# Sparse attention and a SiLU feed-forward layer on one Trainium2 core: batch 3's preparation at the places of batch 2, its four x transposes from ScalarE

## The chip, the cores and the metric

The kernel runs on one core of a Trainium2 chip. Its engines are TensorE (PE, with PEld for the loading of weights), VectorE (DVE), ScalarE (ACT), GpSimd (POOL) and SyncE (SP, which here only issues DMAs). An engine name with a q (ACTq, SPq) is that engine's instruction queue, where the issuing of a DMA shows. The metric is device time in microseconds (us) of one execution. All times "in the trace" are counted from the start of the profiled execution's span.

## The reference, cut to what matters

Four batches, 8 heads, 768 positions, head size 64. Each position attends to the keys less than 16 positions away and to 24 block keys (the maximum over 32 keys), whose values are block means; the output goes through a feed-forward layer with SiLU.

```python
k_sum = k.reshape(B, H, nb, block, D).max(axis=3)      # block 32, nb 24
v_sum = v.reshape(B, H, nb, block, D).mean(axis=3)
scores_l = scale * np.matmul(q, k.transpose(0, 1, 3, 2))
mask_l = np.abs(pos[:, None] - pos[None, :]) < 16
scores_s = scale * einsum(q, k_sum) + np.log(block)
a = softmax(concatenate([where(mask_l, scores_l, -1e9), scores_s]))
x = np.matmul(a, concatenate([v, v_sum]))              # (3072, 512)
h = x @ w_in                                           # 512 -> 2048
out = (h * sigmoid(beta * h)) @ w_out                  # 2048 -> 512
```

## The kernel before, in words

The batches go one after the other, and each has two **stages** on PE. The *h stage* is `x @ w_in` (16 tiles of 128 features, L600), with ACT's Silu behind each tile (L611). The *product stage* is the product with `w_out`, done by a seven-product scheme (L664, products numbered 1 to 7) for three row tiles t = 0, 1, 2: 21 products of 8 matmuls each. VectorE makes sums of h for it (L645).

The attention of batch b is **prepared inside the product stage of batch b-1**, in pieces slipped between the products. Heads are worked in four pairs, g = 0 to 3. The pieces, with their names in the table `AT` that gives their places, are:

- `exp`: a tiny Exp on a dummy tile that brings ACT's exp table in (L743), and `silu`, the same for the Silu table (L740); `ACT_TABLE_LOAD` in the trace.
- `sc`: 24 score matmuls for a pair and a half of the positions (L436), into `big[2]` or `big[1]`, then ACT's exp of them into a tile `e` (L447).
- `mk`: VectorE's multiplication of `e` with the window mask (L451).
- `vm`: 28 matmuls that make the block sums of v (L486) into the bank `scope["c"]` (acc in the trace), with small copies by DVE and ACT to `vm_sb`.
- `sp`: the spread, copies of `vm_sb` into the value tiles `ve` and `vo`; for pairs 0 and 1 by DVE (L371), for 2 and 3 by ACT (L368).
- `av`: 48 matmuls for a pair (L511) into `big[1]` (g even) or `big[2]` (g odd), then DVE's normalization into `xn` (L537, L538).
- `xd`: the transpose of `xn` into `xT`, by a DMA (L553). The table `xq` chooses who issues it: a number above 0 SP, a number from -1 to 0 ACT.

The bank `one[0]` is worth knowing: products 1 and 2 are accumulated in it, ACT copies each result out (L368: `p<-one` for product 1, `o_sb<-one` for product 2), and the h stage puts its tile 3 into `one[0]` and `one[1]` (the first matmuls of line 600 that write `one`).

```python
587     def h_bank(i, kk):
...
589         if i == 3:
590             return one[kk][:, 0, 0:HS]
...
690         elif n == 2:
691             part["lo"] = op.tile([P, d_model], f32, name="o_sb", tag="o_sb")
692             act_cp(part["lo"][:, 0:DH], src)
```

The order is written out by hand. `main` is a list of PE's steps: the h steps of batch 2 are 84 to 99, its products 100 to 120, and batch 3's h steps begin at 121. The products of batch 1 are 63 to 83, so a place of batch 2's preparation plus 37 is the same place for batch 3. `AT` gives each piece a number, and `run` slips it in behind the step of that whole number; between pieces of one step the smaller number goes first.

```python
553         (nc.sync if AT[f"xq{b}"][g] > 0 else nc.scalar).dma_start_transpose(...)
...
747         for i, f in enumerate(main):
748             f()
749             while sides and sides[0][0] < i + 1:
750                 sides.pop(0)[1]()
```

Every engine takes its instructions strictly in this written order. The recording layer adds the semaphore waits. A DMA's completion is a semaphore called DMAHW0 to DMAHW7, taken in turn by the DMAs of SP and ACT.

Of the kernel before, what the change touches and what calls it, by code (L numbers as in the profile page):

```python
# [65 lines left out]
    'qd3': [91.148, 91.216, 90.659, 93.011],  # L66
    'vc3': [95.284, 91.652, 97.814, 103.191],
    'vo3': [97.047, 94.075, 98.896, 104.362],
    'exp3': [100.49],
    'sc3': [101.05, 101.06, 104.012, 104.199, 106.253, 106.263, 107.654, 107.71],  # L70
    'mk3': [102.2, 102.9, 107.921, 107.97, 106.952, 108.221, 108.907, 110.666],
    'silu3': [112.501],
    'vm3': [107.308],
    'sp3': [107.454, 109.9, 110.9],
    'av3': [110.088, 110.664, 114.187, 114.973],
    'xd3': [111.756, 114.644, 117.265, 117.799],
    'hs3': [126.972, 131.206, 132.732, 134.708, 136.323],
    'xq1': [-0.443, -0.159, -0.972, -0.722],
    'xq2': [-0.681, -0.396, -0.684, -0.009],
    'xq3': [-0.996, -0.83, 0.5, -0.341],  # L80
    'mask2': [46.27],
}

# [887 lines left out]
```

## Time and profile before

| | us |
|---|---|
| median of 3 runs | 212.68 (211.92 to 213.24) |
| the profiled execution, its own time | 211.17 |
| its span, first to last instruction | 209.5 |
| PE busy | 201.5 (96%) |
| DVE, ACT, POOL busy | 138.2, 124.8, 64.0 |

The granted TensorE clock was 0.992 on average. The profile's view of the chain of waits follows the work that ended last back from the end of the span, and names at each step what released it. The timeline view gives start and duration of each group of like instructions of an engine; a bracket behind it gives the idle time ahead of it and what ended that.

### The profile page before, as it was taken

The page shows a single profiled execution, that of the slowest core. Times are in us where ns is not written, and L with a number is a line of the kernel's source. Part 1 is how long each engine was busy: PE and PEld are TensorE (multiplying, and loading weights), DVE is VectorE, ACT ScalarE, POOL GpSimd, SP SyncE. Part 2 cuts the span into 40 slices and gives each one's busy share as a digit, 9 for nine tenths or more (in the row PEclk, how much of TensorE's full clock was granted, in tenths as well). Part 3 has the DMA queues.
Part 4 walks back from the last instruction along what each step waited for, and adds up shares of the span by engine and source line. Part 5 has one row for each costly group of instructions (what it writes and reads, how often), then busy time and mean ns, then how long its engine had stood idle before and what let it go on. Part 6 is the DMA issues. An engine that isn't in the chain of part 4 may idle for free.

```text
span 209.5 us, 5777 instructions
## 1 busy us (share of the span) xinstructions
PE 201.5 (96%) x2387; PEld 139.8 (67%) x2387; DVE 138.2 (66%) x314; ACT 124.8 (60%) x189; POOL 64.0 (31%) x95
## 2 busy tenths in 40 slices
PE   7899999999999999999999999999999899999993
PEld 2478656656455775556888865568788656568882
DVE  4568674899889981859999523999699304464132
ACT  2438876689777114867978229669895039662210
POOL 7708990101820036530520072453501100000111
PEclk9969999999999999999999999999999999999999
DMA  6999999999969999999989979999525530000242
GB/s 121 190 223 170 181 187 188 207 207 202 184 160 231 228 227 258 226 175 206 129 217 242 201 211 288 178 200 189 133 96 102 150 103 3 0 0 3 100 100 100
DMA packets 79193, 34.12 MB, mean 163 GB/s; under 512 B 61488, under 2 KB 76224, under 8 KB 79168
## 3 DMA queue, kind: packets, MB, share of 16 engines
q1 hardware_dynamic: 62768, 24.12, 56.4%
q0 software_dynamic: 7424, 7.34, 22.0%
q10 hardware_dynamic: 8976, 2.30, 7.6%
q8 instruction: 18, 0.29, 0.6%
q14 instruction: 7, 0.06, 0.1%
HBM read 27.37 MB, written 6.29 MB: 161 GB/s over the span
## 4 chain that ended last, share of the span: by engine, by line
PE 82%; DVE 8%; DMA 3%; issue 2%; ACT 2%; ACTq 1%; POOL 1%; POOLq 0%
PE big L600 28%; PE one L664 15%; PE acc L664 11%; PE big L578 5%; PE one L615 4%; PE one L584 3%; DMA qrow<-in_q_dram 3%; PE big L384 3%; PE one L600 2%; DVE s_sb L645 2%; PE big L511 2%; PE big L584 2%; DVE xn L538 1%; PE big L436 1%; PE big L422 1%
## 5 line engine op out<-in xcount | busy, mean ns | idle before, releaser
L600 PE MATMUL big<-xT,w_in_sb 128*128 128x384 bf16 x360 | 60.5, 326 | 0.0
L600 PEld LDWEIGHTS <-w_in_sb 128*128 128x128 bf16 x384 | 37.6, 98 | 26.1 <-issue 1.9
L611 ACT ACTIVATE h_sb<-big,beta_sb 128x768 bf16<-128x768 f32 x45 | 39.6, 905 | 23.2 <-PE big L600 23.1
L664 PEld LDWEIGHTS <-h_sb 128*128 128x128 bf16 x320 | 30.7, 98 | 4.7 <-issue 0.2
L645 POOL TENSOR_TENSOR o_sb<-p,u 128x256 f32<-128x256 f32 x10 | 7.3, 730 | 86.9 <-DVE u L645 76.3
L447 ACT ACTIVATE e<-big,bias 128x768 bf16<-128x768 f32 x32 | 27.4, 900 | 6.1 <-PE big L426 3.6
L664 PE MATMUL one<-w_out_sb,h_sb 128*128 128x256 bf16 x240 | 30.3, 273 | 0.3 <-DVE u L645 0.2
L664 PEld LDWEIGHTS <-s_sb 128*128 128x128 bf16 x240 | 23.1, 98 | 3.3 <-issue 0.5
L645 DVE TENSOR_TENSOR s_sb<-h_sb 128x768 bf16<-128x768 bf16 (+2 forms) x16 | 7.8, 488 | 24.8 <-ACT h_sb L611 24.8
L645 DVE TENSOR_TENSOR u<-one,p 128x256 f32<-128x256 f32 x20 | 8.4, 420 | 17.2 <-PE one L664 17.2
L456 POOL CAST ve<-vst 128x832 bf16<-128x832 f32 (+2 forms) x16 | 15.3, 965 | 14.5 <-DMA vst<-in_v_dram 14.5
L368 ACT COPY o_sb<-one 128x256 f32<-128x256 f32 (+1 forms) x14 | 6.1, 433 | 15.8 <-PE one L664 5.7
L451 DVE TENSOR_TENSOR e<-e,mask 128x768 bf16<-128x768 bf16 x24 | 13.9, 603 | 2.2 <-ACT e L447 2.0
L615 PE MATMUL one<-w_out_sb,h_sb 128*128 128x512 bf16 x64 | 15.0, 380 | 0.0
L365 POOL COPY kw<-km 128x288 bf16<-128x288 bf16 x12 | 7.6, 635 | 21.4 <-DVE km L357 11.5
L361 DVE TENSOR_REDUCE km<-kT 128x24 bf16<-128x768 bf16 x12 | 11.3, 944 | 1.9 <-ACT kT L368 1.9
L538 DVE TENSOR_TENSOR xn<-big,r 128x768 bf16<-128x768 f32 x12 | 11.5, 957 | 0.4
L578 PE MATMUL big<-xT,w_in_sb 128*128 128x384 bf16 x64 | 11.4, 326 | 0.0
L368 ACT COPY p<-acc 128x256 f32<-128x256 f32 x10 | 3.8, 376 | 11.9 <-PE acc L664 7.7
L664 PE MATMUL acc<-t_sb,h_sb 128*128 128x256 bf16 x80 | 10.9, 273 | 0.0
L568 POOL CAST qn<-qst 128x768 bf16<-128x768 f32 x8 | 7.4, 934 | 10.4 <-DMA qst<-in_q_dram 7.0
L664 PE MATMUL one<-t_sb,s_sb 128*128 128x256 bf16 x80 | 10.4, 273 | 0.1
(145 smaller groups left out, 318.0 us busy)
## 6 DMA issues: line engine op xcount, KB each, us to landing
out_dram<-o_sb SPq DMA_DIRECT2D x19, 256.0 KB, 3.2
vst<-in_v_dram SPq DMA_DIRECT2D x13, 336.0 KB, 5.0
kst<-in_k_dram SPq DMA_DIRECT2D x8, 384.0 KB, 5.3
qst<-in_q_dram SPq DMA_DIRECT2D x8, 384.0 KB, 4.7
w_in_sb<-in_moe_w_in_dram POOLq DMA_DIRECT2D x4, 512.0 KB, 7.1
w_out_sb<-in_moe_w_out_dram POOLq DMA_DIRECT2D x4, 512.0 KB, 13.7
vo<-ve SPq DMA_DIRECT2D x12, 107.2 KB, 2.4
vst<-in_v_dram SPq DMA_DIRECT2D x3, 416.0 KB, 7.8
```

The costliest lines, as they stand in the source:

```text
L361: nc.vector.tensor_reduce(out=km[g][:, NK:NK + nb], in_=kT[g][:, W:W + S].rearrange("p (n f) -> p n f", f=block), op=ALU.max, axis=AX.X)
L447: nc.scalar.activation(out=e[:], in_=s[:, :, 0:HS], func=ACTF.Exp, bias=bias[:, 0:1], scale=scale)
L451: nc.vector.tensor_mul(out=e.rearrange("p h (m q) -> p h m q", q=QT), in0=e.rearrange("p h (m q) -> p h m q", q=QT), in1=(mask2 if b > 1 e ...
L456: eng.tensor_copy(out=ve[:, g, lo:hi, 0:D], in_=vst[g][:, lo:hi])
L538: nc.vector.tensor_mul(out=x[:, 3 * us[0]:3 * us[0] + 3 * n].rearrange("p (k j) h d -> p k (j h) d", k=n), in0=tv[:, :, :, 0:D], in1=r[:, ...
L578: nc.tensor.matmul(t[:, 0:HS], w_in_sb[:, ki, i * P:(i + 1) * P], xT[:, ki, 0:HS], start=(ki == 0), stop=(ki == k1 - 1))
L584: nc.tensor.matmul(t[:, 0:HS], w_in_sb[:, ki, i * P:(i + 1) * P], xT[:, ki, lo:lo + HS], start=(ki == 0), stop=(ki == k1 - 1))
L600: nc.tensor.matmul(o, w_in_sb[:, ki, i * P:(i + 1) * P], x, start=(ki == 0), stop=(ki == k1 - 1))
L611: nc.scalar.activation(out=o, in_=t, func=ACTF.Silu, scale=beta_sb[:, i:i + 1])
L615: nc.tensor.matmul(t[:, 0:hi - lo], h_sb[:, n, ms * P:(ms + 1) * P], w_out_sb[:, n, lo:hi], start=(n == 0), stop=(n == k2 - 1))
L645: eng.tensor_tensor(out=o, in0=a, in1=b, op=op)
L664: nc.tensor.matmul(SLOTS[n], a[:, j, t * P:(t + 1) * P], b[:, j], start=(j == 0 and n not in (2, 3, 7)), stop=(j == J2 - 1), skip_group_ch ...
```

## The change

Only numbers of `AT` for batch 3 change. Each new number of `exp3` to `xd3` is batch 2's number plus 37, and `xq3` becomes a copy of `xq2`.

```diff
-    'exp3': [100.49],
...
-    'mk3': [102.2, 102.9, 107.921, 107.97, 106.952, 108.221, 108.907, 110.666],
-    'silu3': [112.501],
-    'vm3': [107.308],
...
-    'av3': [110.088, 110.664, 114.187, 114.973],
-    'xd3': [111.756, 114.644, 117.265, 117.799],
+    'exp3': [99.362],
...
+    'mk3': [101.907, 104.547, 106.019, 106.041, 107.656, 107.74, 109.6, 109.7],
+    'silu3': [120.261],
+    'vm3': [106.738],
...
+    'av3': [110.1, 110.251, 113.15, 113.759],
+    'xd3': [110.535, 112.753, 114.844, 117.713],
...
-    'xq3': [-0.996, -0.83, 0.5, -0.341],
+    'xq3': [-0.681, -0.396, -0.684, -0.009],
```

The order on each engine shows what that moves. First place: ACT at the end of batch 2's product stage, from the second half of the spread to the copy that frees `one[0]` (`one_78` here; `p` and `o_sb` are the copies of products, `xT<-xn` the x transposes). Before:

```order
L368 COPY ve<-vm_sb 32x2x6x64 [waits DMAHW6_49,DMAHW0_49]
L368 COPY ve<-vm_sb 32x2x6x64
L368 COPY o_sb<-one_78 128x256 [waits DMAHW5_49,DMAHW4_49,PE_49]
L553 DMA_TRANSPOSE xT<-xn 128x6x128 [waits DMAHW3_49,DMAHW2_49,DMAHW4_49,DMAHW1_49,DVE_49]
L740 ACT_TABLE_LOAD
L740 ACTIVATE dummy<-bias 128x1
L368 COPY p_2930<-one_78 128x256 [waits DVE_49,PE_49]
L553 DMA_TRANSPOSE xT<-xn 128x6x128 [waits DMAHW7_49]
L368 COPY p_3007<-acc_2550 128x256 [waits PE_49,Pool_49]
L553 DMA_TRANSPOSE xT<-xn 128x6x128 [waits DMAHW3_49,DMAHW2_49,DVE_49]
L368 COPY o_sb<-one_78 128x256 [waits PE_49]
```

And with the change:

```order
L368 COPY ve<-vm_sb 32x2x6x64 [waits DMAHW6_49,DMAHW0_49]
L368 COPY ve<-vm_sb 32x2x6x64
L553 DMA_TRANSPOSE xT<-xn 128x6x128 [waits DMAHW3_49,DMAHW2_49,DMAHW4_49,DMAHW1_49,DVE_49]
L368 COPY o_sb<-one_78 128x256 [waits DMAHW5_49,PE_49]
L553 DMA_TRANSPOSE xT<-xn 128x6x128 [waits DMAHW5_49,DVE_49]
L368 COPY p_2986<-one_78 128x256 [waits DVE_49,PE_49,Activation_49]
L553 DMA_TRANSPOSE xT<-xn 128x6x128 [waits DMAHW2_49,DVE_49]
L368 COPY p_3007<-acc_2551 128x256 [waits PE_49,Pool_49]
L553 DMA_TRANSPOSE xT<-xn 128x6x128 [waits DMAHW3_49,DVE_49]
L368 COPY o_sb<-one_78 128x256 [waits PE_49]
L740 ACT_TABLE_LOAD
```

There were three transposes in this queue and are now four; the first stands ahead of the copy of product 2 (t = 1) and no longer behind it; the table load for Silu went from the middle to the end. Second place: SP at the same time, among the stores of the output.

```order
 L679 DMA out_dram<-o_sb 64x512 x4
-L553 DMA_TRANSPOSE xT<-xn 128x6x128
 L679 DMA out_dram<-o_sb 128x512 x4
```

SP's transpose (pair 2) is the one that went to ACT. With its waits, the row of before reads as follows on SP; DMAHW4 and DMAHW7 are those of the transposes of pairs 0 and 1 on ACT, and DMAHW2 is its own, on which ACT's transpose of pair 3 waits above:

```order
L553 DMA_TRANSPOSE xT<-xn 128x6x128 [waits DMAHW4_49,DMAHW2_49,DMAHW7_49,DVE_49,PE_49]
```

With the change no such row is left on SP. Third place: DVE in the same stage, from the sums of products of t = 0 to the normalization of pairs 0 and 1 (`e<-e,mask` are the masks, `vm_sb` the block sums, `vo`, `ve` the spread). Before:

```order
L451 TENSOR_TENSOR e<-e,mask_176 128x768
L371 CAST vm_sb<-acc_2549 32x2x64 x2
L371 COPY vo<-vm_sb 32x2x6x64 x2
L371 COPY ve<-vm_sb 32x2x6x64 x2
L451 TENSOR_TENSOR e<-e,mask_176 128x768 x2
L645 TENSOR_TENSOR u_2801<-one_79,p_2725 128x256
L451 TENSOR_TENSOR e<-e,mask_176 128x768 x2
L537 RECIPROCAL r<-big_80 128x12
L538 TENSOR_TENSOR xn<-big_80,r 128x768
L537 RECIPROCAL r<-big_81 128x12
L538 TENSOR_TENSOR xn<-big_81,r 128x768
L451 TENSOR_TENSOR e<-e,mask_176 128x768
```

And with the change:

```order
L451 TENSOR_TENSOR e<-e,mask_176 128x768 x2
L371 CAST vm_sb<-acc_2550 32x2x64 x2
L451 TENSOR_TENSOR e<-e,mask_176 128x768 x2
L371 COPY vo<-vm_sb 32x2x6x64 x2
L371 COPY ve<-vm_sb 32x2x6x64 x2
L645 TENSOR_TENSOR u_2774<-one_79,p_2758 128x256
L451 TENSOR_TENSOR e<-e,mask_176 128x768 x2
L537 RECIPROCAL r<-big_80 128x12
L538 TENSOR_TENSOR xn<-big_80,r 128x768
L537 RECIPROCAL r<-big_81 128x12
L538 TENSOR_TENSOR xn<-big_81,r 128x768
```

Two masks moved ahead of the spread, one mask ahead of the block sums, and the last mask from behind the normalization of pair 1 to ahead of that of pair 0. On PE the scores of pair 3 go one step later (behind step 108, from 107), the block sums one step earlier (106, from 107), and the AV of pairs 2 and 3 one step earlier (113, from 114); all else on PE keeps its step.

More of the change, by code (lines that the diff above doesn't have):

```diff
@@ L68 @@
     'vo3': [97.047, 94.075, 98.896, 104.362],
-    'exp3': [100.49],
-    'sc3': [101.05, 101.06, 104.012, 104.199, 106.253, 106.263, 107.654, 107.71],
-    'mk3': [102.2, 102.9, 107.921, 107.97, 106.952, 108.221, 108.907, 110.666],
-    'silu3': [112.501],
-    'vm3': [107.308],
-    'sp3': [107.454, 109.9, 110.9],
-    'av3': [110.088, 110.664, 114.187, 114.973],
-    'xd3': [111.756, 114.644, 117.265, 117.799],
+    'exp3': [99.362],
+    'sc3': [101.902, 101.912, 104.132, 104.349, 106.423, 106.507, 108.144, 108.507],
+    'mk3': [101.907, 104.547, 106.019, 106.041, 107.656, 107.74, 109.6, 109.7],
+    'silu3': [120.261],
+    'vm3': [106.738],
+    'sp3': [107.773, 109.1, 110.3],
+    'av3': [110.1, 110.251, 113.15, 113.759],
+    'xd3': [110.535, 112.753, 114.844, 117.713],
     'hs3': [126.972, 131.206, 132.732, 134.708, 136.323],
```

## The prediction

> **What bounds the kernel now.** PE is busy in 96% of the span, so time can only be won where PE stands still. I first read the chain of waits in order of time around the end of the stage that the change touches, batch 2's products, because a gap there is on the path to the end. These are its pieces (start, length, engine, tile and line):
>
> ```profile
> 165.69 0.44 DVE o_sb L645
> 166.13 1.26 ACTq L553
> ...
> 167.43 0.38 ACT o_sb L368
> ...
> 167.86 0.81 PE one L600 x4
> ```
>
> PE ends the products and begins batch 3's h stage at 165.49, but its third tile needs the bank `one[0]`, and ACT's copy that frees it (`o_sb`, the last product 2) comes only at 167.43, behind a DMA issue of line 553. The view of waits has the stall in one row, PE's only one between 141 and 174:
>
> ```profile
> PE one L600 <- ACT o_sb L368: 0.9, 1, 0.9
> ```
>
> How much time it costs is read better from two equal stretches: the first 34 matmuls of the h stage, once in batch 2, which the change leaves alone, and once in batch 3 (first number: length):
>
> ```profile
> 121.36:126.73 5.37, 5.36 (x34) 1.00 0.76 221
> 165.49:171.93 6.44, 5.53 (x34) 1.00 0.40 113
> ```
>
> The same work at the same granted clock (1.00) takes 6.44 - 5.37 = **1.07 us** longer in batch 3.
>
> Why was the issue late? The view of line 553 lists the issues and the semaphore waits ahead of them (durations in ns, shortest/median/longest, then first and last start). First the stage of batch 2's preparation, all four transposes on ACT, then that of batch 3's, three on ACT and one on SP:
>
> ```profile
> L553 ACTq DMA_TRANSPOSE xT<-xn x4: 1226/1261/1862, 113.1 to 118.5; - x4
> L553 ACTq EVENT_SEMAPHORE  x3: 17/17/17, 114.5 to 118.5; - x3
> ...
> DMA to landing us min/median/max: 3.5/5.3/5.8
> ```
>
> ```profile
> L553 ACTq EVENT_SEMAPHORE  x3: 38/38/3801, 156.8 to 162.3; - x3
> ```
>
> ACT's queue stood for 3.80 us on one semaphore, from 162.3 to 166.1. The chain names DVE's `o_sb` sum as releaser, but that sum is written behind the transpose in program order, and the recording layer can't wait for what comes later. The order names another: pair 3's transpose on ACT waits for DMAHW2, the completion of pair 2's on SP. That one was issued and landed so:
>
> ```profile
> 163.25 1.24 SPq L553 DMA_TRANSPOSE xT<-xn  x1
> ```
>
> ```profile
> xT<-xn SPq DMA_TRANSPOSE x1, 2.8
> ```
>
> ```profile
> SPq L553 <- DMA xT<-xn: 0.4, 1, 0.4
> ```
>
> 163.25 + 2.8 = 166.05, just when ACT goes on; and SP's own issue had waited for a transpose of ACT to land. So each change of queue between two transposes costs a whole landing, and behind the second one stands the copy for which PE waits.
>
> The Trainium skill ("DMA: Bandwidth & Descriptors", Silent corruption: two transposing streams in flight at once) says that transposes from SP and from ACT are two streams and that the later stream must wait for the full completion of the earlier. By that rule four transposes from one queue need no such wait; the 17 ns of batch 2 agree, and the sum by it is the one below.
>
> **The change part by part.** Batch 2's stage and batch 3's stage have the same pieces, and the change copies the places, so the rows of batch 2 price nearly everything, shifted by 142.33 - 98.15 = 44.18 us:
>
> ```profile
> 98.15 0.93 PE L664 MATMUL acc<-t_sb,h_sb 128*128 128x256 bf16 x7
> ```
>
> ```profile
> 142.33 0.93 PE L664 MATMUL acc<-t_sb,h_sb 128*128 128x256 bf16 x7
> ```
>
> *The fourth transpose on ACT.* It adds one issue of 1.23 to 1.86 us to ACT and takes one of 1.24 off SP, where only stores stand behind it. ACT in batch 2's stage:
>
> ```profile
> 113.11 1.23 ACTq L553 DMA_TRANSPOSE xT<-xn  x1
> 114.44 0.37 ACT L368 COPY o_sb<-one 128x256 f32<-128x256 f32 x1 [0.54 <-PE acc L664]
> ...
> 116.49 1.86 ACTq L553 DMA_TRANSPOSE xT<-xn  x1
> ...
> 118.53 1.23 ACTq L553 DMA_TRANSPOSE xT<-xn  x1
> 119.81 0.37 ACT L368 COPY o_sb<-one 128x256 f32<-128x256 f32 x1 [0.98 <-PE one L664]
> 120.20 1.28 ACT L740 ACT_TABLE_LOAD   x1
> 121.49 0.20 ACT L740 ACTIVATE dummy<-bias 128x1 f32<-128x1 f32 x1
> 125.78 2.48 ACT L611 ACTIVATE h_sb<-big,beta_sb 128x768 bf16<-128x768 f32 x3 [4.08 <-PE big L600]
> ```
>
> Shifted: the last transpose is issued at 162.71, the copy that frees `one[0]` runs from 163.99 to 164.36. PE wants the bank 1.30 us behind the start of the h stage, as here in batch 2 (122.66 against 121.36):
>
> ```profile
> 122.66 0.81 PE L600 MATMUL one<-xT,w_in_sb 128*128 128x384 bf16 x4
> ```
>
> The copy ended 2.48 us ahead of that. So the stall of 1.07 goes whole: **-1.07**. Landings: the last transpose, issued at 162.71 with the longest landing of 5.8, is there at 168.5. Its first reader is the 25th matmul, 24 x 0.1625 = 3.9 us behind the start (eight take 1.30), at about 169.4. **0**; the cover is 0.9 us.
>
> *The Silu table load at the end.* 1.28 + 0.20 us of ACT, hidden in the 4.08 us for which ACT then waits for the first h tile: **0**. Without that cover it would cost at most 1.48.
>
> *Masks, spread, AV.* DVE gets up to 2 x 0.55 us of masks ahead of the spread, and one mask ahead of the normalizations. The rows are of batch 2 (AV of pair 2, end of `xn` of pair 1) and then of batch 3 before (`xn` of pair 1, last mask):
>
> ```profile
> 114.35 0.22 PE L511 MATMUL big<-ve,e 128*64 128x65 bf16 x1
> ```
>
> ```profile
> 113.26 0.96 DVE L538 TENSOR_TENSOR xn<-big,r 128x768 bf16<-128x768 f32 x1
> ...
> 157.58 0.96 DVE L538 TENSOR_TENSOR xn<-big,r 128x768 bf16<-128x768 f32 x1
> 158.46 0.55 DVE L451 TENSOR_TENSOR e<-e,mask 128x768 bf16<-128x768 bf16 x1
> ```
>
> AV of pair 3 needs `big[2]`, free when `xn` of pair 1 is done: 158.40 by batch 2's rows; 158.54 + 0.55 = 159.09 by batch 3's own rows with the extra mask. PE comes to that AV half a pair behind 158.53, at 158.97. So 0 by one way, 0.12 by the other; I take **0**, since DVE's queue is now batch 2's row for row.
>
> *Block sums a step earlier.* They go to 106.07 + 44.18 = 150.25. They need the last cast of v (POOL) and bank acc, freed by the first of two sums of DVE:
>
> ```profile
> 106.07 0.58 PE L486 MATMUL acc<-ve,A_avg 128*32 128x128 bf16 x28
> ```
>
> ```profile
> 146.91 1.23 POOL L456 CAST ve<-vst 128x832 bf16<-128x832 f32 x1
> ```
>
> ```profile
> 149.43 0.77 DVE L645 TENSOR_TENSOR o_sb<-acc,u 128x256 f32<-128x256 f32 x2
> ```
>
> Ready at 148.14 and at about 149.8: **0**, with 2.1 and 0.4 us to spare. The scores of pair 3 go later, away from their inputs: 0. The exp table load keeps its place in ACT's order: 0.
>
> *Length of the stage.* Both stages by the view of windows (length, PE busy):
>
> ```profile
> 98.15:121.36 23.21, 23.12 (x390) 19.72 (x389) 19.27 (x42) 16.59 (x27) 5.00 (x7) 1.00 1.10 200
> 142.33:165.49 23.16, 23.16 (x390) 19.66 (x388) 18.02 (x44) 16.43 (x27) 5.30 (x8) 1.00 0.66 139
> ```
>
> PE is busy in all 23.16 us now, so no order of the pieces can shorten it, and batch 2's order took 23.21: **+0.05**, between 0 and +0.2 with the 0.12 above.
>
> **Sum:** -1.07 + 0.05 = -1.02 us. The profiled execution goes from a span of 209.5 to 208.5 and from 211.17 to 210.15. That execution was quicker than all three timed runs (211.92 to 213.24), so I carry the difference, not the level, to their median: 212.68 - 1.02 = 211.66, or **211.7 us**, half a per cent faster.
>
> **The rivals.** *ACT's issue takes the place of the wait: no gain.* The second issue of 1.24 us no longer runs on SP, and if ACT's queue were full at the end, the copy for `one[0]` would come that much later: -1.02 + 1.24 = +0.22, so 212.9. For it: with the change ACT issues pair 2's and pair 3's transposes right ahead of that copy. Against it: in batch 2 that copy stood 0.98 us waiting for PE, and ended 2.48 us before the bank was wanted. The Trainium skill ("DMA: Bandwidth & Descriptors", Issuing engines are not separate DMA queues) says that issuing from several engines saves the sequencer's issue time and nothing else; by that rule alone the change would be a loss, of this rival's size.
>
> *A transpose holds ACT at its first place: slower.* Pair 0's transpose now stands ahead of the copy of product 2 (t = 1), which frees `one[0]` for product 1 (t = 2) in PE's queue:
>
> ```profile
> 115.23 1.05 PE L664 MATMUL one<-w_out_sb,h_sb 128*128 128x256 bf16 x8
> ```
>
> In batch 2 the copy ends at 114.81, only 0.42 us ahead. Were pair 0's transpose held as long as pair 3's was (3.80), PE would stand 3.4 us, and the sum would be -1.02 + 3.4 = +2.4: 215.1. From 1.44 us of delay on (0.42 + 1.02) the change is a loss. For it: that transpose still waits on four DMA semaphores in the order, and DVE reaches `xn` of pair 0 one mask later than before. Against it: with the change no transpose is left on SP in this stage, and the same place in batch 2 cost nothing.
>
> **How the numbers follow.** The forecast gets 0.82, no gain 0.10, slower by the first transpose 0.05, and 0.03 is left for what I don't see. A measurement of this kernel tells about 1%, or 2.1 us, from no change; the forecast's 0.5% is less, so it is mostly "within 1%". More than 1.07 isn't there to win, so faster by over 1% comes only from the spread of the runs (1.3 us over three): 0.07. Slower by over 1% is the third case and a little spread: 0.06. Within 1%: 0.87. The range starts at the lowest run less the gain, 211.92 - 1.07, and half a microsecond of spread below, 210.4, and ends at the highest run with no gain, 213.2.
>
> **What would show it.** In the profile of the changed kernel: no stall of PE on `one` at line 600, and the first 34 matmuls of batch 3's h stage in about 5.4 us; four issues of line 553 on ACT with semaphore waits well under 1 us; the copy `o_sb` ending over 2 us before its bank is wanted; batch 2's product stage 23.1 to 23.4 us long. The prediction is wrong if PE waits at an AV (L511), at the block sums (L486) or at product 1 of t = 2, or if the stall at line 600 stays.

## The result and the profile after

The changed kernel is faster, by less than one per cent: a median of 210.9 us over 21 runs (209.61 to 212.84) against 211.68 us over 21 runs of before (210.94 to 217.3). The ratio is 0.9943 with a 95% interval from 0.9922 to 0.9964, so 0.6% or 1.2 us, where half a per cent was forecast. The medians alone are 0.8 us apart; unlike them, the ratio leaves out slow runs, among them the changed kernel's two of 212.75 and 212.84 us, in which the granted clock was 0.976. The profiled span went from 209.5 to 208.3 us.

The view of waits names no stall of PE on another engine any more from 120 us to the end. Where the time came from shows when the span from the start of batch 2's products on is cut into three stretches: these products, the first 34 matmuls of batch 3's h stage, and the rest. First before, then the changed kernel (length, PE busy, count, granted clock, DMA share, GB/s):

```profile
142.33:165.49 23.16, 23.16 (x390) 1.00 0.66 139
...
171.93:209.50 37.57, 34.10 (x264) 1.00 0.14 43
sum 67.17, PE 62.78; mean PE 20.93
```

```profile
142.34:165.41 23.07, 23.07 (x390) 1.00 0.83 147
165.41:170.79 5.38, 5.37 (x35) 1.00 0.29 103
170.79:208.30 37.51, 34.10 (x264) 0.99 0.14 43
sum 65.96, PE 62.53; mean PE 20.84
```

The middle stretch went from 6.44 to 5.38 us (-1.06), the product stage from 23.16 to 23.07 (-0.09), the rest from 37.57 to 37.51 (-0.06). Together -1.21. Ahead of the first cut the two executions don't differ: both reach it at 142.3. That is luck, as the last section shows; this sum from the cut to the end is the finer measure of what the change did, and I use it for the experiments too.

The queue of ACT in the changed kernel, by the timeline and the view of line 553, reads as batch 2's did; between them stands PE's first use of the bank `one[0]` in the h stage:

```profile
162.28 1.51 ACTq L553 DMA_TRANSPOSE xT<-xn  x1
163.86 0.37 ACT L368 COPY o_sb<-one 128x256 f32<-128x256 f32 x1 [1.29 <-PE one L664]
164.25 1.28 ACT L740 ACT_TABLE_LOAD   x1
165.55 0.20 ACT L740 ACTIVATE dummy<-bias 128x1 f32<-128x1 f32 x1
169.84 2.48 ACT L611 ACTIVATE h_sb<-big,beta_sb 128x768 bf16<-128x768 f32 x3 [4.09 <-PE big L600]
```

```profile
166.71 0.81 PE L600 MATMUL one<-xT,w_in_sb 128*128 128x384 bf16 x4
```

```profile
L553 ACTq EVENT_SEMAPHORE  x3: 17/17/17, 158.5 to 162.2; - x3
...
DMA to landing us min/median/max: 2.8/3.9/4.9
```

The longest semaphore wait recorded in this view fell from 3801 to 17 ns. The copy for `one[0]` now waits for PE (1.29 us), not PE for it, and ends at 164.23, 2.48 us before PE takes the bank at 166.71.

### The profile page after: what moved, and what is told of

The parts are those of the page before. It is cut to its first block, busy times and chain, and to the rows that moved or that the text cites. A ratio compares the mean times of both kernels' runs of the same rounds, so it can differ in the third digit from the quotient of the medians.

```text
span 208.3 us, 5772 instructions
## 1 busy us (share of the span) xinstructions
PE 200.2 (96%) x2383; PEld 138.8 (67%) x2387; DVE 137.9 (66%) x314; ACT 124.7 (60%) x189; POOL 62.7 (30%) x95
## 4 chain that ended last, share of the span: by engine, by line
PE 60%; DMA 15%; DVE 13%; POOL 5%; issue 3%; SPq 2%; ACT 2%; POOLq 0%
PE big L600 28%; PE one L664 15%; PE acc L664 11%; DMA vst<-in_v_dram 6%; DMA w_out_sb<-in_moe_w_out_dram 5%; DMA krow<-in_k_dram 3%; DVE kw L371 3%; DVE w_out_sb L337 2%; PE one L600 2%; DVE s_sb L645 2%; PE big L511 2%; DVE xn L538 1%; PE big L436 1%; DVE km L357 1%; POOL w_in_sb L331 1%
## 5 line engine op out<-in xcount | busy, mean ns | idle before, releaser
L456 POOL CAST ve<-vst 128x832 bf16<-128x832 f32 (+2 forms) x16 | 14.8, 935 | 16.1 <-DMA vst<-in_v_dram 14.2
L615 PE MATMUL one<-w_out_sb,h_sb 128*128 128x512 bf16 x61 | 14.5, 380 | 0.4 <-issue 0.3
L451 DVE TENSOR_TENSOR e<-e,mask 128x768 bf16<-128x768 bf16 x24 | 13.3, 583 | 1.7 <-ACT e L447 1.6
L365 POOL COPY kw<-km 128x288 bf16<-128x288 bf16 x12 | 6.8, 565 | 22.3 <-DVE km L357 12.4
```

Source lines behind the costliest of these rows:

```text
L451: nc.vector.tensor_mul(out=e.rearrange("p h (m q) -> p h m q", q=QT), in0=e.rearrange("p h (m q) -> p h m q", q=QT), in1=(mask2 if b > 1 e ...
L456: eng.tensor_copy(out=ve[:, g, lo:hi, 0:D], in_=vst[g][:, lo:hi])
L615: nc.tensor.matmul(t[:, 0:hi - lo], h_sb[:, n, ms * P:(ms + 1) * P], w_out_sb[:, n, lo:hi], start=(n == 0), stop=(n == k2 - 1))
```

## The experiments

My theory was that the queues of the transposes made the stall: each change of queue waits for a landing, and ACT's queue, held by that wait, keeps back the copy that PE needs. The rivals were that the moved pieces brought the gain, or that the late landing of pair 3's transpose was what PE would have paid anyway. All measurements stand in one table; the stretches are those of the cut, in us, from one profiled execution each, the ratio to before is from the timed runs.

| kernel | products | 34 matmuls | rest | sum | ratio (95% interval) |
|---|---|---|---|---|---|
| before | 23.16 | 6.44 | 37.57 | 67.17 | 1 |
| the change | 23.07 | 5.38 | 37.51 | 65.96 | 0.9943 (0.9922 to 0.9964) |
| e1 queue only | 23.15 | 5.38 | 37.48 | 66.01 | 0.9953 (0.993 to 0.9976) |
| e2 places only | 23.07 | 5.82 | 37.57 | 66.46 | 0.9973 (0.9947 to 1.0) |
| e3 two and two | 23.16 | 5.38 | 37.54 | 66.08 | 0.9956 (0.9925 to 0.9988) |
| e4 behind the copy | 23.15 | 6.56 | 37.54 | 67.25 | 1.0014 (0.9988 to 1.004) |
| e5 pair 1 from SP | 23.67 | 5.38 | 37.52 | 66.57 | 0.9939 (0.9914 to 0.9963) |
| e6 two ahead of the copy | 23.97 | 5.37 | 37.49 | 66.83 | 0.9995 (0.9963 to 1.0027) |
| e7 all from SP | 23.07 | 5.38 | 37.49 | 65.94 | 0.9937 (0.991 to 0.9963) |

The timed intervals of the change, e1, e2, e3, e5 and e7 all overlap, so timing alone doesn't tell these kernels apart; the sums do, as far as one execution of each goes. The column of the rest, in which all nine run the same code, spreads from 37.48 to 37.57, so I read nothing into differences of sums below 0.1 us.

**e1, the queue alone.** Before, with the one row of queues changed:

```diff
-    'xq3': [-0.996, -0.83, 0.5, -0.341],
+    'xq3': [-0.681, -0.396, -0.684, -0.009],
```

> Before with only xq3 changed (all four x transposes of batch 3 from ScalarE, all other places as before). Theory A (the gain is the change of queue: no transpose waits for one of another queue, so the copy that frees one[0] isn't held): the semaphore wait ahead of the transposes on ACT falls from 3.80 us to under 0.1; pair 2's and pair 3's transposes are issued back to back from 162.3, the copy ends at 165.5 to 166.0, ahead of the 166.8 at which PE wants the bank; first 34 matmuls of batch 3's h stage 5.4 us; 1.07 us faster, ratio 0.995. Theory B (the moved pieces bring the gain): the stall stays, 6.4 us for the 34 matmuls, ratio 1.000. Theory C (ACT's issue takes the place of the wait): the copy still ends after 167, ratio 0.999 or above.

ACT's timeline, PE's first use of the bank and the waits of line 553:

```profile
162.78 2.75 ACTq L553 DMA_TRANSPOSE xT<-xn  x2
165.58 0.37 ACT L368 COPY o_sb<-one 128x256 f32<-128x256 f32 x1 [2.50 <-PE one L664]
```

```profile
167.24 0.81 PE L600 MATMUL one<-xT,w_in_sb 128*128 128x384 bf16 x4
```

```profile
L553 ACTq EVENT_SEMAPHORE  x4: 17/28/38, 157.2 to 164.2; - x4
```

The two transposes go back to back for 2.75 us, and the copy still comes in time: it ends at 165.95, and PE takes the bank at 167.24. The stall is gone (5.38), and 1.16 of the 1.21 us of the whole change are there. Theory B, that the places bring it, and theory C, that ACT's issue takes the wait's place, both fall.

**e2, the places alone.** The changed kernel with the queues of before:

```diff
-    'xq3': [-0.681, -0.396, -0.684, -0.009],
+    'xq3': [-0.996, -0.83, 0.5, -0.341],
```

> The changed kernel with xq3 as before (pair 2's transpose from SP again), all places new. Theory A: the two crossings of queues stay, but pair 1's transpose is now issued at 158.6 and no longer at 159.5, so pair 2's on SP goes at about 162.3, lands at 165.1, pair 3's on ACT is issued until 166.4, and the copy ends at about 166.8 against the 166.7 at which PE wants the bank: the wait on ACT stays long (2.5 to 3 us) but the stall shrinks to 0 to 0.3; 0.8 to 1.1 us faster than before, ratio 0.995 to 0.996. Theory B (places alone do it, the wait on ACT was no matter): the same ratio but with no long wait on ACT. If the queue alone decides: stall of 0.9 as before, ratio 1.000.

The waits of line 553 and PE's timeline:

```profile
L553 ACTq EVENT_SEMAPHORE  x4: 17/38/3228, 156.1 to 164.0; - x4
```

```profile
168.96 0.81 PE L600 MATMUL one<-xT,w_in_sb 128*128 128x384 bf16 x4 [0.28 <-ACT o_sb L368]
```

The long wait on ACT stays (3.23 us, longer than the 2.5 to 3 expected), and the stall shrinks from 0.90 to 0.28 us of idle, the stretch from 6.44 to 5.82: counted from the start of the products, the places let pair 1's transpose start 0.9 us sooner and the two behind it 0.7, so the chain of landings ends sooner. The stall is within theory A's range, at its upper end, the gain of 0.71 us in the sum just below it. Timed, the ratio's interval just reaches 1. So by these sums the places are worth 0.71 us when they stand alone, and less than 0.1 beside the queue (e1 against the change): the two parts buy the same stall, and their gains don't add.

This run also settles who released ACT. The timeline and the waits view name DVE's `o_sb` sum again, with 4.2 us, but here the three times differ:

```profile
164.38 1.28 SPq L553 DMA_TRANSPOSE xT<-xn  x1
```

```profile
167.26 1.23 ACTq L553 DMA_TRANSPOSE xT<-xn  x1
```

```profile
167.08 0.76 DVE L645 TENSOR_TENSOR o_sb<-acc,u 128x256 f32<-128x256 f32 x2
```

ACT goes on at 167.26, while DVE's first sum ends only at about 167.5. SP's transpose, with its landing of 2.8 us, was there at 167.18. So the landing released it.

**e3, two and two.** Before, with pair 3 also from SP, so one crossing of queues is left and ACT isn't held by it:

```diff
-    'xq3': [-0.996, -0.83, 0.5, -0.341],
+    'xq3': [-0.996, -0.83, 0.5, 0.341],
```

> Before with pair 3's transpose also from SP (pairs 0 and 1 from ACT, 2 and 3 from SP); places as before. Theory A (what costs is ACT's queue held ahead of the copy, not a crossing of queues as such): SP still waits for ACT's landing and issues pair 2 at 163.2, pair 3 right behind at 164.5, landed by 167.3 to 168.8, ahead of its first reader at 169.4; ACT copies at 163.9; no stall; 1.07 us faster, ratio 0.995. Rival (each crossing costs a landing on the path): the SP transposes are late, PE waits for a DMA at line 600, ratio 0.998 to 1.002.

ACT's copy, and SP's two transposes:

```profile
165.93 0.37 ACT L368 COPY o_sb<-one 128x256 f32<-128x256 f32 x1 [1.32 <-PE one L664]
```

```profile
165.15 2.60 SPq L553 DMA_TRANSPOSE xT<-xn  x2
```

No stall (5.38), the sum 1.09 us below before. A crossing as such costs PE nothing when what stands behind the held transpose isn't wanted soon: on SP those are stores.

**e4, pair 3's transpose behind the copy.** Before, with one number changed, so that the copy isn't held but the transpose is as late as it was:

```diff
-    'xd3': [111.756, 114.644, 117.265, 117.799],
+    'xd3': [111.756, 114.644, 117.265, 118.9],
```

> Before with pair 3's transpose written behind the copy that frees one[0] on ACT (place 118.9 for 117.799), queues and all else as before. Theory A: the copy runs at 163.9, no stall on the bank; the transpose is still issued at 166.1 after SP's landing and lands 2.8 to 4.3 us later, 168.9 to 170.4, while its first reader comes at 169.4: a stall of 0 to 1.0 us on that DMA is left; 0.1 to 1.07 us faster, most likely 0.7, ratio 0.995 to 0.9995. Rival (the late landing of pair 3 was the cost all along, the copy only looked guilty): no gain, 34 matmuls still 6.4 us, ratio 1.000.

ACT's timeline, PE's timeline:

```profile
165.36 0.37 ACT L368 COPY o_sb<-one 128x256 f32<-128x256 f32 x1 [1.32 <-PE one L664]
167.50 1.28 ACTq L553 DMA_TRANSPOSE xT<-xn  x1
```

```profile
168.20 0.81 PE L600 MATMUL one<-xT,w_in_sb 128*128 128x384 bf16 x4
...
171.99 1.14 PE L600 MATMUL big<-xT,w_in_sb 128*128 128x384 bf16 x6 [1.02 <-DMA xT<-xn]
```

The copy is early, PE takes the bank without a wait at 168.20, and then stands 1.02 us on the landing of pair 3's transpose, issued 4.49 us before. The stretch is 6.56, no better than before, and the ratio 1.0014 holds no gain. The rival's number was right here, and my "most likely 0.7" wrong.

But the rival's reason, that this landing was the cost all along, doesn't fit the trace of before. There the same transpose, issued at 166.12, landed in 3.3 us, at 169.4. That is 1.0 us ahead of the matmul that reads it first (the third of the row that begins at 170.13), and just when that matmul would have come without the stall (165.49 + 3.9). In e4 it took 4.4 us. The view of line 553, for this one transpose, of before and of e4:

```profile
L553 ACTq DMA_TRANSPOSE xT<-xn x1: 1276/1276/1276, 166.1 to 166.1; - x1
...
DMA to landing us min/median/max: 3.3/3.3/3.3
```

```profile
L553 ACTq DMA_TRANSPOSE xT<-xn x1: 1281/1281/1281, 167.5 to 167.5; - x1
...
DMA to landing us min/median/max: 4.4/4.4/4.4
```

The row of PE in before that holds the first reader, and SP's wait for ACT's copy there:

```profile
170.13 1.46 PE L600 MATMUL big<-xT,w_in_sb 128*128 128x384 bf16 x8
```

```profile
SPq L679 <- ACT o_sb L368: 1.2, 1, 1.2
```

What moved beside the transpose is the last store on SP, of before and of e4:

```profile
167.83 0.34 SPq L679 DMA_DIRECT2D out_dram<-o_sb  x1
```

```profile
168.08 0.36 SPq L679 DMA_DIRECT2D out_dram<-o_sb  x1
```

This store needs ACT's copy too, and in before it waited for it. So it went 1.71 us behind the transpose in before, and 0.58 us behind it in e4. That the earlier store made the landing longer is likely, but no run shows it by itself. What e4 does show: with the copy freed, the late transpose became the next wait and cost as much as the first one had; that the two are of one length is chance. Freeing the copy alone is worth nothing. The queue change pays because it also has pair 3's transpose issued earlier (at 164.3 in e1, where its first reader comes at about 169.8).

**e5, a crossing elsewhere.** The changed kernel with pair 1 from SP:

```diff
-    'xd3': [110.535, 112.753, 114.844, 117.713],
+    'xd3': [110.545, 110.535, 114.844, 117.713],
...
-    'xq3': [-0.681, -0.396, -0.684, -0.009],
+    'xq3': [-0.681, 0.396, -0.684, -0.009],
```

> The changed kernel with pair 1's transpose from SP (ACT, SP, ACT, ACT). Theory (a crossing costs a landing, and what stands behind the held transpose in its queue pays): SP waits for pair 0's landing (157.2 + 2.8 to 4.9), ACT's transpose of pair 2 for pair 1's landing 2.8 to 4.4 later, so it goes at about 163.7 and holds the copy p of product 5, whose bank acc PE wants at 164.5 for product 3: a stall of 0 to 3.7 us at line 664 on acc, most likely 0.8, so about 0.8 us slower than the changed kernel and 0.4 faster than before, ratio 0.998 (0.994 to 1.01). Rival (only the crossing right ahead of the last copy counts): no new stall, ratio 0.9945.

The three issues that follow each other's landing, on ACT and on SP, and PE's rows:

```profile
158.59 1.23 ACTq L553 DMA_TRANSPOSE xT<-xn  x1
...
164.35 1.36 ACTq L553 DMA_TRANSPOSE xT<-xn  x1
165.81 0.37 ACT L368 COPY p<-acc 128x256 f32<-128x256 f32 x1 [3.52 <-PE one L664]
```

```profile
161.48 1.28 SPq L553 DMA_TRANSPOSE xT<-xn  x1
```

```profile
151.62 0.58 PE L486 MATMUL acc<-ve,A_avg 128*32 128x128 bf16 x28 [0.27 <-DVE o_sb L645]
...
164.28 1.91 PE L664 MATMUL one<-w_out_sb,h_sb 128*128 128x256 bf16 x16
166.23 1.03 PE L664 MATMUL acc<-w_out_sb,s_sb 128*128 128x256 bf16 x8
```

158.59, 161.48, 164.35: two crossings, 2.9 us each. The copy of product 5 is held, to 166.18, and PE's product 3 starts at 166.23, where it would have been due at 166.03 (product 2 and 7 began at 164.28 and take 1.75). That is 0.2 us, not 0.8: both landings were as short as any seen. The mechanism is as told, its size missed, and the forecast ratio of 0.998 lies outside the interval; 0.2 us is a tenth of a per cent, too little for the timed runs to show. The stage's other 0.4 us lies mostly earlier, in a wait of 0.27 us at the block sums, on DVE's sum of t = 0, and about 0.1 ahead of product 7. The edit has no part in that, since all transposes come later: DVE was behind because one copy for `kw` (L371) took 1.14 us in this execution and 0.45 in the changed kernel's. The 0.4 us that the prediction saw to spare at the block sums wasn't there.

**e6, the slower rival in small.** The changed kernel with pair 1's transpose also ahead of the first copy:

```diff
-    'xd3': [110.535, 112.753, 114.844, 117.713],
+    'xd3': [110.535, 110.545, 114.844, 117.713],
```

> The changed kernel with pair 1's transpose also ahead of the copy of product 2 (t = 1) on ACT, all four from ACT: the slower rival of the prediction at its first place, in small. Theory: pair 1's transpose waits for its normalization (158.3), is issued until 159.8, the copy ends at about 160.2, and PE wants the bank for product 1 (t = 2) at 159.3: a stall of about 0.9 us at line 664 on one, released by ACT's o_sb; about 0.3 us faster than before, ratio 0.9985. Rival (that copy has slack, as no wait showed there): no stall, ratio 0.9945.

ACT's timeline, PE's timeline:

```profile
159.89 2.58 ACTq L553 DMA_TRANSPOSE xT<-xn  x2
162.50 0.37 ACT L368 COPY o_sb<-one 128x256 f32<-128x256 f32 x1 [1.83 <-DVE r L537]
```

```profile
162.93 1.03 PE L664 MATMUL one<-w_out_sb,h_sb 128*128 128x256 bf16 x8 [0.84 <-ACT o_sb L368]
```

0.84 us of stall where 0.9 was expected, the sum 0.87 above the changed kernel, and timed no gain is left over before (0.9995). The prediction's third case names a real edge: at its first place the copy has about 0.4 us to spare, and one more issue of 1.25 us in front of it uses that up.

**e7, all four from SP.** The changed kernel with the other single queue:

```diff
-    'xq3': [-0.681, -0.396, -0.684, -0.009],
+    'xq3': [0.681, 0.396, 0.684, 0.009],
```

> The changed kernel with all four transposes from SP. Theory (one queue, whichever, is what counts): no transpose waits for another queue, ACT's copies are never held; pairs 2 and 3 go at about 163 and 164.5, behind stores, and land by 167.5 to 168.9, ahead of the first reader at 169.3; same time as the changed kernel, ratio 0.994 to 0.996. Rival (ACT's issue time was on the path): faster than the changed kernel by up to 1.2 us, ratio 0.989. Third way (SP's stores hold the transposes): PE waits for a DMA at line 600, up to 1 us, ratio 0.995 to 0.9995.

SP's timeline:

```profile
163.90 1.27 SPq L553 DMA_TRANSPOSE xT<-xn  x1
165.28 1.18 SPq L679 DMA_DIRECT2D out_dram<-o_sb  x2
166.56 2.61 SPq L553 DMA_TRANSPOSE xT<-xn  x2
```

The sum is 65.94 against 65.96: which of the two queues has all four doesn't matter. The Trainium skill ("DMA: Bandwidth & Descriptors", Issuing engines are not separate DMA queues) says that issuing from several engines saves only the time of the issue. The trace agrees in so far as ACT's four issues, gone here, bought no time. But the rule isn't all there is to the choice of the engine: e1 changes nothing but which engine issues one transpose, and gains 1.16 us, since a wait goes.

## Why the prediction was right, point by point

- **The stall goes whole (-1.07): right**, -1.06 measured, and e1 shows that the queue alone does it. **The reason was half of it.** The prediction blamed the held copy and gave the landing of pair 3's transpose a cost of 0 with the change, which was true with the change; it didn't ask what the late transpose would cost if the copy alone were freed. e4 measured it: 1.02 us. The rows of before show that nothing was to spare: issued at 166.12 and landed in 3.3 us, it was there at 169.4, and without the stall its first reader comes at 169.4; with 4.3, the longest landing of that stage, it would have been 170.4.
- **Who released ACT: right against the waits view**, shown by e2. The rule cited for it (the Trainium skill, "DMA: Bandwidth & Descriptors", Silent corruption: two transposing streams in flight at once) is that the later stream waits for the full completion of the earlier. The traces agree: waits of 3.23 and 3.80 us at a crossing into ACT with pair 3 held in front, 38 ns at most on one queue in e1. They show the wait only; no run here lets two such streams overlap.
- **The length of the stage (+0.05): wrong, also in sign**; -0.09 measured. The step that failed is "PE is busy in all 23.16 us now, so no order of the pieces can shorten it". All kernels with the old places have 23.15 or 23.16, the change, e2 and e7 have 23.07. Most of it shows at product 1 (t = 2) of before. ACT's copy, and PE's rows, of before:

```profile
157.97 0.37 ACT L368 COPY o_sb<-one 128x256 f32<-128x256 f32 x1
```

```profile
157.45 1.04 PE L664 MATMUL acc<-w_out_sb,s_sb 128*128 128x256 bf16 x8
158.39 1.03 PE L664 MATMUL one<-w_out_sb,h_sb 128*128 128x256 bf16 x8
```

  Eight matmuls usually follow eight by 0.87 us, here by 0.94: PE waited 0.07 us for the copy that ended at 158.34, too little to show as idle beside the modelled ends. It began 0.05 us behind the end of that copy, just as it did in the stall (167.81 and 167.86). With the new places AV stands in between. The other 0.02 I have no row for. By the same step "More than 1.07 isn't there to win" fell: the first two stretches of the cut alone have 1.15.
- **Silu table, masks, spread, AV, block sums (0 each): right** as far as the sum shows; the change and e1, which has none of them, differ by 0.05 us in all. (The 48 matmuls that the list of pieces gives to the AV of a pair are those of two pairs, 24 each; so what the sum calls half a pair, 0.44 us, is a whole one, and its 158.97 for pair 3 stands.)
- **The rival "ACT's issue takes its place"**: fell with e1 and e7. **The slower rival**: its price held in e6 (0.84 for 0.9), its condition didn't come about in the change.
- **The level: 0.8 us off.** 211.7 was forecast from three runs with a median of 212.68; over 21 runs before is at 211.68, and the change at 210.9, inside the range of 210.4 to 213.2. The difference, -1.0 forecast, is -1.2 by the ratio and by the cut, -0.8 by the medians.

## What to carry to other kernels

Keep DMA transposes that follow each other closely on one queue: a change of queue between two of them cost a landing, 2.8 to 3.8 us here, and everything behind the held one in its queue waited too. If there must be one, let it fall on a queue with nothing urgent behind it, as in e3. When a stall is traced to one late instruction, ask what would have been late next if it hadn't been, and what the fix sets going; in e4 the next wait took the whole gain. Two edits that shorten the same stall don't add up.

## What was not expected of the hardware

- **The start of the program spreads more than the change is worth.** The same code reaches batch 2's products at 142.33 us in one execution and at 145.16 in another; the nine profiles lie between. PE's waits in that part differ from run to run, on the first loads as in this row of the waits view of e6, or on nothing that the profile shows as in that of e2; the granted clock is below 1 early in some of them (0.90 over the first 50 us in e7, 1.00 in the change):

```profile
PE big L384 <- DMA qrow<-in_q_dram: 1.9, 2, 1.7
```

```profile
PE big L422 <- issue: 1.6, 1, 1.6
```

  From that point to the end, the four kernels in which the view shows no stall of PE (the change, e1, e3, e7) agree within 0.14 us. What makes the start differ was not tried.
- **The same transpose landed in different times.** Four from SP (e7) took 2.8 to 3.1 us, four from ACT 2.8 to 4.9 in the changed kernel. They are issued at other moments beside other stores, so the queue is not shown to be the cause. One difference goes with the places: pair 0's transpose landed in 4.3 to 4.5 us in the four kernels in which ACT loads the Silu table 1.3 us behind its issue (before, e1, e3, e4), and in 2.7 to 2.8 us in the five in which the load comes last. No run moves that load alone.
